# Loading batch 1 of a retention-and-mixer kernel through the casting software DMA queue, with ch2 weights queued later, ch1 of both halves first and u of batch 1 by crossbar

## The chip, the cores and the metric

One core of a Trainium2 chip. The time is the device time of one execution in microseconds; lower is better. Runs are compared with runs of the kernel before that were made on the same chip in the same job. Engines: PE is TensorE, DVE VectorE, ACT ScalarE, POOL GpSimd, SP SyncE. Lines are given as L with the number in the kernel's file; the changed kernel's numbers are 3 to 9 higher than those of the kernel before. "At half rate" or "cold" is said of TensorE's array when matmuls start twice as far apart as usual; the granted clock is the profile's column for it (1.00 is full, 0.50 half). A hole is a gap in TensorE's work beyond the usual spacing of its matmuls.

## The reference

A retention layer (a decayed running sum of k times v, read out by q) on 4 batches of 8 heads, 768 steps, head size 64, and then a token mixer and a channel mixer on the 512 joined channels:

```python
for t in range(S):
    state = gamma[None, :, None, None] * state + einsum('bhd,bhe->bhde', k[:, :, t], v[:, :, t])
    y[:, :, t] = scale * einsum('bhd,bhde->bhe', q[:, :, t], state)
# x: y with its heads joined, (4, 768, 512)
h  = maximum(xt @ w_tok1, 0) @ w_tok2        # xt: x transposed, d_tok = 256
u  = x + h transposed
h2 = maximum(u @ w_ch1, 0) @ w_ch2           # d_ch = 1536
return u + h2
```

Matrix products run in fp16 with fp32 sums.

## The kernel before

Everything is an `Op` with an estimated duration; `arrange()` puts all Ops in an order by these estimates, and the order on each engine is then fixed in the program. Per batch there are four `front` stages (one for each pair of heads: the retention, the token mixer, u) and one `back` (ch1 and ch2, the two matrix products of the channel mixer, each for two halves of the sequence). The back of batch b fills TensorE while the fronts of batch b+1 run. Batch 0's front has nothing to hide behind.

In batch 0 the rows come through the software queue, issued by GpSimd, which casts q and v to fp16 on the way. In later batches they come as fp32 through SyncE's queue, and GpSimd casts q and v:

```python
def load(nm):
    ...
    eng = nc.gpsimd if first and p else nc.sync
    dma = eng.dma_start(out=t, in_=rows.rearrange("h (c p) d -> p (h c) d", p=P))
    if b == 1:
        tc.add_manual_dep(dma.ins, wops["c1", 1].ins.ins.name, ...,
                          reason="the weights come first")
def cast(slot, nm):
    if first:
        ... return nc.gpsimd.dma_start(out=t, in_=...)      # casts
    ld = load(nm)
    ... nc.gpsimd.tensor_copy(t, src.tile...)
# ... cut
after = {(3, "v"): (("t1", 0), ("t2", 0))}
for p in range(NP):
    front(0, p)
queue += [wops[w] for w in (("c1", 0), ("c1", 1), ("c2", 0))]
```

What GpSimd does in each front: the fp16 copy of x (two halves), the triangular mask on some of the score tiles, and the fp16 copy of u (two halves):

```python
nc.gpsimd.tensor_copy(X16.tile[:, half(hf)], X.tile[:, half(hf), pc])          # x cast
nc.gpsimd.affine_select(out=M.tile, in_=M.tile, compare_op=ALU.is_ge, ...)     # mask
nc.gpsimd.tensor_copy(u, X.tile[:, half(hf), pc])                              # u cast
```

The scheduler models how many DMAs may be open on a queue, with one entry for each Op:

```python
RING = dict(SP=3, POOL=8)
if op.dma and len(ring[op.eng]) >= RING[op.eng]:
    start = max(start, ring[op.eng][-RING[op.eng]])
```

## Time and profile before

| | kernel before |
|---|---|
| time, median of 4 runs | 207.12 us (206.38 to 207.40) |
| the traced run | 205.84 us, span 204.1 us |
| TensorE busy | 192.3 us, 94% of the span |
| first ch1 matmul of batch 0 | 33.66 us |
| hole of TensorE at k of batch 1 | 2.98 us beyond the usual spacing |
| from the first ch1 matmul to the last matmul | 167.2 us |
| last add and store | 3.2 us |

The time is the sum of three: when ch1 begins, how long the rest takes on TensorE (the dense part), and the tail. The lines for this are in the prediction, which starts from 207.16, the median of the first three of the four runs.

### The profile page before, as it was taken

The numbers are of one execution on the slowest core, as the hardware profiler recorded it, in microseconds if no ns is written. First come the engines' busy times: TensorE is split into PE (matmuls) and PEld (weight loads), VectorE is DVE, ScalarE is ACT, GpSimd is POOL, SyncE is SP. The second block draws the span as 40 slices with busy tenths as digits, with TensorE's granted clock in tenths as the row PEclk, the third lists the DMA queues.
The fourth block names the chain that finished last, engine by engine and source line by source line (L and its number), as shares of the span: only waits on it lengthen the run. The fifth ranks groups of instructions, "written<-read, shape, count | busy, mean of one in ns | idle before, by whom it ended". The sixth has DMA issues, their size and how long they took to land.

```text
span 204.1 us, 4737 instructions
## 1 busy us (share of the span) xinstructions
PE 192.3 (94%) x1900; PEld 118.8 (58%) x1900; DVE 112.6 (55%) x285; ACT 97.4 (48%) x211; POOL 69.2 (34%) x116
## 2 busy tenths in 40 slices
PE   6598999769999999999999999999999999999993
PEld 2354796444577766676646656566557545545552
DVE  7499863016698889896296545947582021021021
ACT  7256797642489642465503650275115604604700
POOL 7998283033145543453442134215132000000000
PEclk9999999999999999999999999999999999999999
DMA  7999999989799999999997999898531112012012
GB/s 114 179 218 186 208 211 206 250 201 262 186 273 215 190 182 231 219 217 169 161 244 173 136 228 237 149 219 133 128 95 51 39 51 103 3 51 103 0 55 103
DMA packets 88470, 32.55 MB, mean 159 GB/s; under 512 B 79328, under 2 KB 84704, under 8 KB 88448
## 3 DMA queue, kind: packets, MB, share of 16 engines
q1 hardware_dynamic: 76128, 25.57, 61.3%
q0 software_dynamic: 12320, 6.69, 23.2%
q8 instruction: 15, 0.25, 0.5%
q14 instruction: 7, 0.06, 0.1%
HBM read 26.74 MB, written 6.29 MB: 162 GB/s over the span
## 4 chain that ended last, share of the span: by engine, by line
PE 81%; DMA 8%; DVE 6%; ACT 2%; issue 1%; POOL 0%; POOLq 0%; DVEq 0%
PE ba L626 31%; PE ba L597 28%; DMA kf<-in_k_dram 5%; PE fa L491 5%; PE fa L512 4%; PE fa L403 4%; DMA v<-in_v_dram 3%; PE fa L440 2%; DVE k L313 2%; PE fa L437 2%; PE fa L361 2%; DVE am L416 1%; PE fa L332 1%; ACT qT L340 1%; DVE U L373 1%
## 5 line engine op out<-in xcount | busy, mean ns | idle before, releaser
L626 PE MATMUL ba<-wc,h 128*128 128x512 f16 (+1 forms) x300 | 68.9, 371 | 0.0
L597 PE MATMUL ba<-uT,wc 128*128 128x384 f16 x384 | 68.2, 326 | 0.0
L610 ACT ACTIVATE h<-ba 128x384 f16<-128x384 f32 x96 | 46.4, 492 | 39.2 <-PE ba L597 38.7
L597 PEld LDWEIGHTS <-wc 128*128 128x128 f16 x384 | 36.0, 98 | 22.5
L626 PEld LDWEIGHTS <-h 128*128 128x128 f16 x300 | 27.2, 98 | 25.6
L635 DVE TENSOR_TENSOR o<-x,ba 128x512 f32<-128x512 f32 (+1 forms) x25 | 16.6, 663 | 42.1 <-PE ba L626 42.0
L416 DVE TENSOR_TENSOR am<-fa,mask 128x384 f16<-128x384 f32 x58 | 29.9, 551 | 11.8 <-PE fa L403 11.7
L468 POOL CAST x<-x 128x384 f16<-128x384 f32 x30 | 15.2, 514 | 28.2 <-issue 12.7
L519 DVE TENSOR_TENSOR x<-x,fa 128x384 f32<-128x384 f32 x28 | 14.5, 551 | 11.6 <-PE fa L512 11.2
L313 DVE TENSOR_SCALAR k<-kf,gk 128x384 f16<-128x384 f32 x32 | 15.8, 534 | 8.5 <-DMA kf<-in_k_dram 8.5
L451 ACT ACTIVATE x<-fa,gy 128x192 f32<-128x192 f32 (+1 forms) x42 | 14.9, 421 | 8.6 <-PE fa L440 8.6
L373 DVE SCALAR_TENSOR_TENSOR U<-U,gp,fa 128x64 f32<-128x64 f32 x64 | 17.5, 276 | 1.1
L292 POOL CAST q<-qf 128x768 f16<-128x768 f32 x12 | 10.2, 849 | 21.4 <-DMA qf<-in_q_dram 20.5
L380 ACT ACTIVATE r<-U 64x320 f16<-64x320 f32 x16 | 7.5, 466 | 20.6 <-DVE U L373 20.6
L530 POOL CAST u16w<-x 128x384 f16<-128x384 f32 x16 | 7.9, 508 | 20.9 <-DVE x L519 20.9
L440 PE MATMUL fa<-v,am 128*128 128x64 f16 x192 | 13.6, 193 | 0.0
L440 PEld LDWEIGHTS <-am 128*128 128x128 f16 x192 | 12.1, 98 | 2.3
L491 PEld LDWEIGHTS <-wt 128*128 128x128 f16 x192 | 11.9, 98 | 2.1
L512 PEld LDWEIGHTS <-wt 128*128 128x128 f16 x192 | 11.8, 98 | 2.2
L292 POOL CAST v<-vf 128x768 f16<-128x768 f32 x12 | 9.9, 827 | 8.6 <-DMA vf<-in_v_dram 7.9
L194 PE MATMUL fa<-zero 128*128 128x512 f16 x37 | 10.7, 423 | 2.2 <-DVE zero L52 1.3
L340 ACT COPY qT<-fa 128x768 f16<-128x768 f16 x8 | 11.5, 1443 | 2.1 <-PE fa L328 1.7
(60 smaller groups left out, 174.4 us busy)
## 6 DMA issues: line engine op xcount, KB each, us to landing
out_dram<-o SPq DMA_DIRECT2D x23, 256.0 KB, 2.3
kf<-in_k_dram SPq DMA_DIRECT2D x13, 384.0 KB, 6.4
qf<-in_q_dram SPq DMA_DIRECT2D x12, 384.0 KB, 5.8
vf<-in_v_dram SPq DMA_DIRECT2D x12, 384.0 KB, 5.3
wc<-in_moe_w_ch_dram POOLq DMA_DIRECT2D x1, 1536.0 KB, 24.3
kf<-in_k_dram POOLq DMA_DIRECT2D x3, 384.0 KB, 6.4
wc<-in_moe_w_ch_dram POOLq DMA_DIRECT2D x1, 1024.0 KB, 16.2
q<-in_q_dram POOLq DMA_DIRECT2D x4, 192.0 KB, 5.9
```

The source lines that it names most:

```text
L292: nc.gpsimd.tensor_copy(t, src.tile.rearrange("p (h c) d -> p h c d", h=2))
L313: (nc.gpsimd if keng == "POOL" else nc.vector).tensor_scalar(k16[:, :, j, :], src, gk[:, h:h + 1], None, ALU.mult)
L373: nc.vector.scalar_tensor_tensor(U[:, c], U[:, c - 1], gp[:, p:p + 1], o, ALU.mult, ALU.add)
L416: nc.vector.tensor_tensor(am, src[:, :HC], mask, ALU.mult)
L440: nc.tensor.matmul(o[:, j * D:(j + 1) * D], AM[2 * hf + j].tile[:, i], V.tile[:, j * NC + c], start=(c == 0), stop=(c == 0 or j == 1))
L468: nc.gpsimd.tensor_copy(X16.tile[:, half(hf)], X.tile[:, half(hf), pc])
L491: nc.tensor.matmul(acc[:, jt * P:(jt + 1) * P], wt1[:, i, jt * P:(jt + 1) * P], X16.tile[:, i], start=(i == 0), stop=(i == NC - 1))
L512: nc.tensor.matmul(acc[:, i * P:(i + 1) * P], wt2[:, jt, t], H1.tile[:, jt], start=(jt == 0), stop=(jt == NJ - 1))
L597: nc.tensor.matmul(acc[:, :SH], w[:, ct, f * P:(f + 1) * P], UT.tile[:, ct, sh * SH:(sh + 1) * SH], start=(ct == 0), stop=(ct == NP - 1))
L610: nc.scalar.activation(H2.tile[:, ft], A.tile[:, :SH], AF.Relu)
L626: nc.tensor.matmul(A.tile[:, :CW], H2.tile[:, ft, i * P:(i + 1) * P], wc2[:, ft, cs], start=(ft == 0), stop=(ft == NF - 1))
L635: nc.vector.tensor_tensor(o[:, :CW], X.tile[:, sh * HC + i, cs], A.tile[:, :CW], ALU.add)
```

## The change

The rows of batch 1 are to come through the casting queue as well. That frees them of the wait for the ch1 weights and of sharing the DMA engines with the ch2 weights, and GpSimd of its casts. The ch2 weights move between the second and third pair of batch 1; batch 0 does ch1 of both halves first, so that these weights are wanted later; u of batch 1 is transposed by a crossbar DMA (one that transposes on the way) and not on TensorE. q of batch 1 leaves the "long" form (three rows in one piece) and becomes two DMAs, one for each head.

```diff
-    LONG, XK, XQ, XU, XBAR = 2, 2, 2, 2, 1500
+    LONG, XK, XQ, XU, XBAR = 1, 2, 2, 1, 1200
-    FILL, TOKBA = 0.75, 2
+    FILL, TOKBA, PRE, TWICE, SOFT = 0.75, 2, 2, 1, 2
+        soft = b < SOFT
-                eng = nc.gpsimd if first and p else nc.sync
+                eng = nc.gpsimd if soft and (b or p) else nc.sync
-                if b == 1:
-                    tc.add_manual_dep(...)
-            if first:
+            if soft:
                 def emit():
                     t = tile_of(slot, sb, [P, 2 * NC, D], F16)
+                    if nm == "q" and b >= LONG:
+                        t = t.rearrange("p (c h) d -> p h c d", h=2)
+                        return [nc.gpsimd.dma_start(out=t[:, h], in_=rows[h].rearrange("(c p) d -> p c d", p=P))
+                                for h in range(2)][-1]
...
+        for part in ((ch1, 0), (ch1, 1), (ch2, 0), (ch2, 1)) if b < TWICE else (...):
+            part[0](part[1])
-    after = {(3, "v"): (("t1", 0), ("t2", 0))}
+    after = {(0, 3, "v"): (("t1", 0), ("t2", 0), ("c1", 0), ("c1", 1))}
+    after[... 1, PRE - 1, "v"] = ... + (("c2", 0),)
-    queue += [wops[w] for w in (("c1", 0), ("c1", 1), ("c2", 0))]
```

Cut: the estimates of some Ops, the order of the k casts, waits that only the scheduler sees, and the form of q's transposes: a q of a software-queue batch that is loaded in the long form is turned on TensorE in 12 matmuls of half width for each pair, any other in 6.

More of the change, by code (lines that the diff above doesn't have):

```diff
@@ L173, in arrange @@
                 shared = min(op.dma, both // 2)
+                if op.eng == "SP" and at > 5000:
+                    at, shared = max(at, free[other]), 0
                 free[mine] = at + op.dma + shared
@@ L210 @@
     weight(("c2", 0), 7800, wc2, moe_w_ch2)
-    queue, sp_done = [], [None]
+    queue, sp_done, kdone = [], [None], []
     x_add, uT_done, y_done, t1_done, t2_done = {}, {}, {}, {}, {}
@@ L256, in emit @@
                     dma = eng.dma_start(out=t, in_=rows.rearrange("h (c p) d -> p (h c) d", p=P))
-                if b == 1:
-                    tc.add_manual_dep(
-                        dma.ins, wops["c1", 1].ins.ins.name,
-                        mybir.DependencyInfo(mybir.DependencyClass.Sync, mybir.DependencyReason.DATA),
-                        reason="the weights come first")
                 return dma
             ns = QLONG if nm == "q" and b < LONG else 1750
-            if first and p:
-                o = Op("POOL", (0,), 1000, 1000, emit, [], [slot], dma=ns)
+            if soft and (b or p):
+                o = Op("POOL", (0,) if first else (2, b, p), 1000, 1000, emit, [], [slot], dma=ns)
                 queue.append(o)
@@ L268, in load @@
                 o = Op("SP", (0, b, p), 100, 100, emit,
-                       deps=[sp_done[-1]] + ([wops["c1", 1]] if b == 1 else []), takes=[slot], dma=ns)
+                       deps=[sp_done[-1], queue[-1] if b == SOFT and p == 0 else None], takes=[slot], dma=ns)
                 sp_done.append(o)
@@ L282, in emit @@
                     return nc.gpsimd.dma_start(out=t, in_=rows.rearrange("h (c p) d -> p (h c) d", p=P))
-                o = Op("POOL", (0,), 1000, 1000, emit, [], [slot], dma=QLONG if nm == "q" else 1400)
+                o = Op("POOL", (0,) if first else (2, b, p), 1000, 1000, emit, [], [slot],
+                       dma=QLONG if nm == "q" and b < LONG else 1400)
                 queue.append(o)
@@ L301, in front @@
                 base=0, pattern=[[0, HC], [1, P]], channel_multiplier=-1)))
-        if first:
-            queue.extend(wops[w] for w in after.get((p, "q"), ()))
+        queue.extend(wops[w] for w in after.get((b, p, "q"), ()))
         vc = cast(V, "v")
-        if first:
-            queue.extend(wops[w] for w in after.get((p, "v"), ()))
+        queue.extend(wops[w] for w in after.get((b, p, "v"), ()))
         def emit():
@@ L315, in front @@
         keng = "POOL" if first and p in KPOOL else "DVE"
-        kc = op(keng, 900, 980, emit, [kl], [K], [KF])
+        kc = op(keng, 900, 980, emit, [kl, kdone[-1] if b else None], [K], [KF])
+        kdone.append(kc)
         KT, QT = Slot("kT"), Slot("qT")
@@ L325, in emit @@
                 for c in range(NC):
-                    if src is Q and first:
+                    if src is Q and soft and b < LONG:
                         for j in range(2):
@@ L332, in emit @@
                     nc.tensor.transpose(tp[:, c * P:(c + 1) * P], o.rearrange("p h d -> p (h d)"), ident16)
-            t = op("PE", 340, 500, emit, [dep, t1_done.get(b * NP - 1) if b > 1 else None], [T], [src])
+            t = op("PE", 340, 500, emit, [dep, t1_done.get(b * NP - 1) if b > 0 else None], [T], [src])
             def emit():
@@ L349, in emit @@
                     in_=src.tile.rearrange("p c h d -> p (c h d)" if src is K else "p c d -> p (c d)"))
-            return Op("SP", (-1, b, p), 100, 100, emit, [dep], [dst], [src], dma=XBAR)
+            return Op("SP", (-1, b, p), 1220, 1220, emit, [dep], [dst], [src], dma=XBAR)
         kt = crossbar(K, KT, kc) if b >= XK else turn(K, KT, kc, "DVE" if first else "ACT")
@@ L362, in emit @@
                                      V.tile[:, j * NC + c], start=True, stop=True)
-        pp = op("PE", 300, 470, emit, [kc, vc, y_done.get(b * NP + p - 2), t1_done.get(b * NP - 1) if b > 1 else None], [ST], [K, V])
+        pp = op("PE", 300, 470, emit, [kc, vc, y_done.get(b * NP + p - 2), t1_done.get(b * NP - 1) if b > 0 else None], [ST], [K, V])
         prev = None
@@ L569, in front @@
             tk = [UT] if (b, "uT") not in uT_done else []
-            e = Op("SP", (-1, b, p), 100, 100, emit, [uc] + ([] if tk else [uT_done[b, "uT"]]), tk,
+            e = Op("SP", (-1, b, p), 1220, 1220, emit, [uc] + ([] if tk else [uT_done[b, "uT"]]), tk,
                    [UW] if tk else [UW, UT], dma=XBAR)
@@ L585, in op, with ch1 @@
             return Op(eng, ((1 if eng == "PE" else 0), b, seq[0]), occ, lat, emit, deps, takes, uses)
-        for sh in range(2):
+        halves = {}
+        def ch1(sh):
             H2 = Slot("h2")
@@ L612, in back, with ch2 @@
                               [A] if ft == 0 else [A, H2]))
+            halves[sh] = H2, rel
+        def ch2(sh):
+            H2, rel = halves[sh]
             for i in range(HC):
@@ L644, in back @@
                     st.prio, st.dma = (-2, b), 800 // parts
-    after = {(3, "v"): (("t1", 0), ("t2", 0))}
+        for part in ((ch1, 0), (ch1, 1), (ch2, 0), (ch2, 1)) if b < TWICE else ((ch1, 0), (ch2, 0), (ch1, 1), (ch2, 1)):
+            part[0](part[1])
+    after = {(0, 3, "v"): (("t1", 0), ("t2", 0), ("c1", 0), ("c1", 1))}
+    after[0 if PRE == 0 else 1, 3 if PRE == 0 else PRE - 1, "v"] = after.get((0 if PRE == 0 else 1, 3 if PRE == 0 else PRE - 1, "v"), ()) + (("c2", 0),)
     for p in range(NP):
         front(0, p)
-    queue += [wops[w] for w in (("c1", 0), ("c1", 1), ("c2", 0))]
     for b in range(1, B):
```

## The prediction

> **What bounds the kernel now.** I read the page first, then the busy times by stretch, the chain of waits, and the timelines of TensorE, GpSimd and SyncE in the first 60 us. The page gives TensorE 192.3 us of the 204.1 us span. By stretch (columns: stretch, its length, busy us of PE, PEld, DVE, ACT, POOL with counts, granted clock, DMA share, GB/s):
>
> ```profile
> 33.60:39.70 6.10, 6.08 (x41) 3.56 (x39) 0.00 (x0) 4.95 (x11) 0.29 (x1) 1.00 1.20 222
> 39.70:42.50 2.80, 0.01 (x1) 0.01 (x1) 0.75 (x2) 0.02 (x1) 0.00 (x0) 1.00 1.01 225
> 42.50:50.00 7.50, 7.50 (x65) 4.11 (x66) 2.52 (x7) 3.72 (x6) 3.31 (x4) 1.00 1.13 231
> 50.00:60.00 10.00, 10.00 (x115) 6.16 (x114) 8.22 (x22) 5.65 (x11) 2.03 (x3) 1.00 0.94 237
> 60.00:140.00 80.00, 80.00 (x895) 52.15 (x893) 58.46 (x143) 38.96 (x86) 32.76 (x57) 1.00 1.09 199
> 140.00:200.94 60.94, 60.90 (x414) 34.37 (x411) 16.63 (x34) 21.62 (x47) 5.29 (x10) 1.00 0.22 65
> ```
>
> The reader is to see three parts. Up to 33.6 us the front of batch 0 runs (a chain of short steps over all engines; ch1 of batch 0 needs all its u). From 33.6 TensorE is full, but for one hole of 2.8 us ending at 42.5. From 42.5 to 200.94 it is busy 158.40 of 158.44 us: nothing can be gained there except by taking matmuls away. The last 3.2 us are the last add and store. So the time is: when the dense part starts, plus the hole, plus the dense work.
>
> The chain of waits names the hole (start, us, what):
>
> ```profile
> 31.27 0.17 DVE x L519
> 31.45 10.21 DMA kf<-in_k_dram
> 41.68 0.76 DVE k L313 x2
> 42.49 0.51 PE fa L332 x6
> ```
>
> The first k rows of batch 1 are issued only when the second piece of the ch1 weights has landed, and then need 10.2 us. The front of batch 0 leans on GpSimd, whose timeline is (start, us, what, idle before):
>
> ```profile
> 12.88 1.54 POOL L203 DMA_DIRECT2D wt<-in_moe_w_tok_dram  x2
> 14.38 1.57 POOL L203 DMA_DIRECT2D wc<-in_moe_w_ch_dram  x2
> 18.85 1.84 POOL L420 TENSOR_SCALAR_AFFINE_SELECT am<-am 128x384 f16<-128x384 f16 x3 [0.87 <-ACT am L414]
> 24.50 0.95 POOL L468 CAST x<-x 128x384 f16<-128x384 f32 x2 [3.81 <-ACT x L451]
> 25.41 1.00 POOL L420 TENSOR_SCALAR_AFFINE_SELECT am<-am 128x384 f16<-128x384 f16 x2
> 26.35 0.50 POOL L468 CAST x<-x 128x384 f16<-128x384 f32 x1
> 28.33 2.09 POOL L530 CAST u<-x 128x384 f16<-128x384 f32 x4
> 31.96 1.93 POOL L530 CAST u<-x 128x384 f16<-128x384 f32 x4 [1.54 <-DVE x L519]
> ```
>
> It has one free gap, 20.7 to 24.5 us; after it come, without slack, the x casts, the masks and the eight u casts, and TensorE begins ch1 right behind (33.66 us in its timeline). Which weights land when, from the list of DMA issues (KB, us to landing):
>
> ```profile
> wc<-in_moe_w_ch_dram POOLq DMA_DIRECT2D x1, 1024.0 KB, 16.2
> wc<-in_moe_w_ch_dram POOLq DMA_DIRECT2D x1, 512.0 KB, 11.7
> ```
>
> The 1024 KB piece (second ch1 weights) is issued at about 15.2 us, so it lands at 31.4.
>
> **What the Trainium skill says.** (1) "DMA: Bandwidth & Descriptors", Queues, rings and completion order: an engine takes turns between queues packet by packet. The trace agrees: the k load took 10.2 us beside the ch2 weights in the other queue, and 3.6 us at best elsewhere. (2) The same page, Anatomy of one DMA: "any semaphore wait happens on the issuing sequencer before dispatch". The trace agrees; SyncE's queue stood with its second load until the weights were in:
>
> ```profile
> 0.81 31.02 SPq L256 DMA_DIRECT2D kf<-in_k_dram  x2
> ```
>
> (3) "TensorE: Matmul & The Clock Gate", Part 1: after about 3.4 us without work the array runs at half rate until some 3.4 us of work have passed. In the trace the first seven filler matmuls start 0.43 us apart, later ones 0.216; the hole of 2.8 us left no slow matmuls behind it. Its granted-clock column shows 1.00 all the same, so it will not show this.
>
> **The change part by part.**
>
> *k, q, v of batch 1 by the software queue.* Removed: the wait on the ch1 weights and the turns with the ch2 weights. In one queue, behind the ch1 weights, the rows of pair 0 come first: batch 0's pairs took 4.0 us each in the DMA records, so k of pair 0 should land near 33 us, v near 36, pair 1 by about 40. The hole should go: -2.98 us (the gap between two starts on TensorE, less the usual 0.16). Also removed: eight GpSimd casts of 0.83 us in batch 1; they sat on no critical step.
>
> Added: DMA issues on GpSimd, in its one instruction stream. k and v cost 1.03 us each in this trace. q, no longer in the long form, is two DMAs of 768 rows; the 768-row token weights cost 0.74, so about 1.5 us for both. A pair is 3.6 us. The built program puts pairs 0 and 1 (about 7 us) before the x cast of pair 1, the one that began at 24.5 us: the first k in the slot of the old ch2 issue, the rest in the 3.8 us gap. Already this overruns the gap by about 2.5 us.
>
> It is worse than that. The software queue's DMAs share eight semaphores in turn, and each issue waits until the DMA eight before it has landed. In the built program's GpSimd order, with waits:
>
> ```
> 36 L279 DMACopy q16_499<-in_q_dram 128x6x64 [waits DMASW4_49]
> 37 L279 DMACopy q16_499<-in_q_dram 128x6x64 [waits DMASW5_49]
> 38 L285 DMACopy v16_528<-in_v_dram 128x12x64 [waits DMASW6_49,PE_49]
> 39 L471 TensorCopy x16_547<-x_304 128x384 [waits Activation_49]
> ```
>
> The v load of pair 1 waits for DMASW6 at 32; its earlier users are q of batch 0's third pair and the 1024 KB weights. So it is issued when those land, at 31.4 us, and the x cast behind it, at 24.5 before, starts after 31.4 + 1.04 = 32.4. (The kernel's own schedule counts the two q DMAs as one and so believes in an earlier one.) From there GpSimd works in order: four x casts and three masks (7 x 0.48 = 3.3, to 35.8), u (0.5), the ch2 issue (1.0), three u (1.5), a k issue (1.0), three u (1.5): the seventh u, which ch1 waited for at about 33.4, is ready at 41.7. TensorE cannot go round it: its stream holds y of pair 2, which needs the first of those masks, next. ch1 starts at about 41.9 instead of 33.66: **+8.3 us**.
>
> *ch2 weights between pairs 1 and 2.* Issued near 36.5 us, they need 11.1 us of queue at most (their packets before: 25.2 to 36.3 in the records' own time, contended), so they land by 48 to 49. ch2 now comes after both ch1 halves: 96 matmuls x 0.163 = 15.6 us plus the front of batch 1 after 41.9, beyond 60. Hidden. Pairs 2 and 3 land by about 56; wanted near 60. Hidden, with 4 us to spare.
>
> *ch1 of both halves first.* The same matmuls in another order: no gain by itself; it buys the ch2 weights 7.8 us. It doubles ACT's share there: 24 relu of 0.49 = 11.8 us beside 15.6 us of ch1, stretched by the front of batch 1. Tight but possible.
>
> *u of batch 1 by crossbar.* 24 transposes leave TensorE, 6 in 0.34 us:
>
> ```profile
> 71.64 0.34 PE fa L543 x6
> ```
>
> -1.35 us, all on the path, as TensorE is full there. Four evictions of 0.8 us leave ACT and four crossbar transfers (3.3 us to landing) enter SyncE's queue.
>
> *q in plain form.* Four qT copies fall from 1.44 to about 0.8 us on ACT; off the path.
>
> **Sum.** -2.98 - 1.35 + 8.3 = +4.0. For new stalls in the static order and a cold array (TensorE idles about 6.5 us ahead of 33.4, over the 3.4 us), +1, an estimate. 207.16 + 5 = 212.
>
> **The rivals.** *A, the intended gain:* GpSimd's stall does not reach ch1, the hole and the transposes go: 207.16 - 4.3 = 202.8. For it: the hole is real. Against: a wait on an issuing queue blocks what stands behind it, as SyncE's 31 us show, and the x cast stands behind it. If only the length of the issues mattered (+2.5, and +2 for the two issues among the u casts), the time would be 207.4. *B, more than I say:* the static order, made for a front that ends sooner, or crossbars of batch 1 behind waiting stores on SyncE, opens holes in the dense part, and the array stays cold into ch1: 1 to 4 us more, 213 to 216. Against: after 41.9 all data of pairs 0 and 1 are in. *C, GpSimd's stall is shorter:* the ch1 weights land earlier, with no load on the other queue. Against: in the kernel before that queue was idle until they had landed too.
>
> **Range and chances.** The certain part is the stall until about 31.4; the x cast is late by 7 to 8, ch1 by 7 to 9. With gains of 3 to 4.3 and 0 to 3 of new holes: 209.9 to 214.9 by the extremes of each, widened below for A. 2% is at 211.3; I am a little above it. Predicted 212.0, range 207.5 to 215.5; faster 0.06, within 2% 0.35, slower 0.59.
>
> **What would show it.** GpSimd's timeline: the v issue standing until about 31.4, the x cast of pair 1 at 32.4, the last u near 42. TensorE: idle from about 27 to 33, ch1 from about 42, no wait for k of batch 1 after it, 158 us of dense work to the end, 24 transposes of u left. I am wrong if the x cast starts before 28, if ch1 starts before 38, or if TensorE shows more than 3 us of holes after ch1 has begun.

## The result

The changed kernel takes 212.04 us (median of 4 runs, 211.68 to 212.25) against 207.12. The ratio is 1.0242, 95% interval 1.0211 to 1.0272: 2.4% slower. A ratio here and below is the mean time of one kernel's runs over that of the other's of the same rounds, so not quite the ratio of the medians that are quoted. Executions over 1.5% slower than the fastest of the same kernel are left out of the means.

GpSimd's timeline of the changed kernel (start, us, what, idle before it and what ended that):

```profile
24.45 0.82 POOL L279 DMA_DIRECT2D q<-in_q_dram  x1 [0.57 <-DMA wt<-in_moe_w_tok_dram]
26.95 0.82 POOL L279 DMA_DIRECT2D q<-in_q_dram  x1 [1.69 <-DMA wc<-in_moe_w_ch_dram]
32.25 1.01 POOL L285 DMA_DIRECT2D v<-in_v_dram  x1 [4.48 <-DMA wc<-in_moe_w_ch_dram]
33.26 0.52 POOL L471 CAST x<-x 128x384 f16<-128x384 f32 x1
...
40.52 1.06 POOL L533 CAST u<-x 128x384 f16<-128x384 f32 x2 [1.23 <-DVE x L522]
42.59 1.85 POOL L533 CAST u<-x 128x384 f16<-128x384 f32 x4
```

The third line is the v load of batch 1's pair 1: GpSimd stood 4.48 us for the second piece of the ch1 weights (1024 KB) before it could issue that load, and 1.69 us for the first piece before the half of q ahead of it. The x cast right behind it had been at 24.50; it is at 33.26. The profile itself names the weights ("DMA wc") as what ended the wait, and so does the chain of waits (start, us, what):

```profile
15.04 16.68 DMA wc<-in_moe_w_ch_dram
...
33.26 0.52 POOL x L471
33.78 0.48 POOL am L423
```

TensorE's timeline in the same stretch:

```profile
26.20 0.19 PE L443 MATMUL fa<-v,am 128*128 128x64 f16 x1
34.30 0.24 PE L443 MATMUL fa<-v,am 128*128 128x64 f16 x1 [7.91 <-POOL am L423]
...
35.93 1.49 PE L494 MATMUL ba<-x,wt 128*128 128x128 f16 x12
...
44.23 0.65 PE L602 MATMUL ba<-uT,wc 128*128 128x384 f16 x3
```

TensorE stands 7.91 us in the middle of y of pair 2, for a mask (L423) that GpSimd does behind that x cast. ch1 begins at 44.23 instead of 33.66. The third line shows twelve matmuls in 1.49 us that took 0.83 before: the array is at half rate. The lines of the kernel before:

```profile
25.43 0.83 PE L491 MATMUL ba<-x,wt 128*128 128x128 f16 x12
33.66 0.65 PE L597 MATMUL ba<-uT,wc 128*128 128x384 f16 x3
```

Busy times by stretch, columns as in the prediction:

```profile
26.20:34.30 8.10, 0.20 (x4) 0.05 (x3) 0.56 (x1) 0.48 (x1) 2.87 (x5) 0.64 1.50 211
34.30:44.23 9.93, 9.37 (x129) 8.86 (x130) 5.33 (x10) 6.14 (x17) 7.92 (x15) 0.78 1.27 138
44.23:207.31 163.08, 163.07 (x1494) 98.66 (x1491) 88.76 (x204) 69.81 (x155) 43.90 (x72) 1.00 0.80 145
```

The granted clock falls to 0.64 and 0.78 in the first two stretches. From 44.23 on TensorE is full: 163.07 busy of 163.08 us, no gap over 0.12 us beyond the usual spacing, no wait for k of batch 1 and none for the ch2 weights. (GpSimd does stand a third time, 0.89 us for the ch2 weights before v of pair 3 at 50.6 us; nothing urgent was behind it.) So the change did what it was for (167.2 us of dense part became 163.1) and lost more than that ahead of it (33.66 became 44.23).

### The profile page after: what moved, and what is told of

It is laid out like the page before. It is cut to its first block, busy times and chain, and to the rows that moved or that the text cites.

```text
span 210.5 us, 4693 instructions
## 1 busy us (share of the span) xinstructions
PE 193.9 (92%) x1878; PEld 119.6 (57%) x1878; DVE 115.4 (55%) x285; ACT 92.6 (44%) x207; POOL 77.6 (37%) x124
## 4 chain that ended last, share of the span: by engine, by line
PE 80%; DMA 11%; POOL 5%; issue 2%; DVE 1%; POOLq 0%; DVEq 0%
PE ba L602 30%; PE ba L635 30%; DMA wc<-in_moe_w_ch_dram 8%; PE fa L494 4%; PE fa L515 4%; DMA v<-in_v_dram 3%; PE fa L406 3%; PE fa L443 3%; PE fa L440 2%; PE fa L364 2%; PE fa L335 1%; POOL kf L260 1%; POOL v L285 1%; POOL u L533 1%; PE ba L515 1%
## 5 line engine op out<-in xcount | busy, mean ns | idle before, releaser
L635 PE MATMUL ba<-wc,h 128*128 128x512 f16 (+1 forms) x300 | 67.5, 371 | 0.0
L644 DVE TENSOR_TENSOR o<-x,ba 128x512 f32<-128x512 f32 (+1 forms) x25 | 16.6, 665 | 43.3 <-PE ba L635 43.1
L533 POOL CAST u16w<-x 128x384 f16<-128x384 f32 x24 | 12.1, 518 | 27.7 <-DVE x L522 27.5
L443 PE MATMUL fa<-v,am 128*128 128x64 f16 x192 | 14.6, 198 | 7.9 <-POOL am L423 7.9
L443 PEld LDWEIGHTS <-am 128*128 128x128 f16 x192 | 13.0, 102 | 10.6 <-POOL am L423 8.1
L315 DVE TENSOR_SCALAR k<-kf,gk 128x384 f16<-128x384 f32 x32 | 17.1, 576 | 0.0
L197 PE MATMUL fa<-zero 128*128 128x512 f16 x42 | 12.2, 426 | 2.6 <-DVE zero L52 1.3
L515 PEld LDWEIGHTS <-wt 128*128 128x128 f16 x192 | 12.5, 101 | 2.4
L502 ACT ACTIVATE h<-fa 128x256 f16<-128x256 f32 x14 | 5.3, 380 | 19.0 <-PE fa L494 19.0
L494 PEld LDWEIGHTS <-wt 128*128 128x128 f16 x192 | 12.4, 102 | 1.8
L440 PE MATMUL fa<-r,qT 128*128 128x128 f16 x80 | 12.8, 227 | 0.3 <-DVE r L390 0.3
L515 PE MATMUL fa<-h,wt 128*128 128x128 f16 x168 | 12.2, 219 | 0.0
```

Of the source, the lines that this page charges most:

```text
L315: (nc.gpsimd if keng == "POOL" else nc.vector).tensor_scalar(k16[:, :, j, :], src, gk[:, h:h + 1], None, ALU.mult)
L440: nc.tensor.matmul(o, QT.tile[:, c * P:(c + 1) * P], R[:, c - 1], start=True, stop=False)
L443: nc.tensor.matmul(o[:, j * D:(j + 1) * D], AM[2 * hf + j].tile[:, i], V.tile[:, j * NC + c], start=(c == 0), stop=(c == 0 or j == 1))
L494: nc.tensor.matmul(acc[:, jt * P:(jt + 1) * P], wt1[:, i, jt * P:(jt + 1) * P], X16.tile[:, i], start=(i == 0), stop=(i == NC - 1))
L515: nc.tensor.matmul(acc[:, i * P:(i + 1) * P], wt2[:, jt, t], H1.tile[:, jt], start=(jt == 0), stop=(jt == NJ - 1))
L635: nc.tensor.matmul(A.tile[:, :CW], H2.tile[:, ft, i * P:(i + 1) * P], wc2[:, ft, cs], start=(ft == 0), stop=(ft == NF - 1))
```

## The experiments

The theory: in the program the DMAs of the software queue take eight completion semaphores in turn (in the trace numbers 103 to 110, over and over), so each issue waits until the DMA eight before it has landed. With q as two DMAs, v of pair 1 stands eight behind the 1024 KB ch1 weights. That wait sits in GpSimd's stream ahead of work that batch 0's front needs. Rivals: the time of the issues on GpSimd (about 1 us each) is the cost; two q DMAs cost by themselves; the cold array; the new order of halves; the crossbars. All twelve kernels gave correct results. The changed kernel's 212.04 was measured in another job than theirs; the kernel before had medians of 207.01 to 207.12 in all four jobs, so times are compared across them. Medians are over all four runs of a kernel; runs 7, 11 and 12 have one slow run each (208.80, 208.72 and 220.84).

| run | time, us (range) | kernel before, us | ratio to before (95%) | first ch1, us |
|---|---|---|---|---|
| changed kernel | 212.04 (211.68 to 212.25) | 207.12 | 1.024 (1.021 to 1.027) | 44.2 |
| 1 one q DMA | 204.00 (203.71 to 204.26) | 207.05 | 0.985 (0.979 to 0.992) | 34.9 |
| 2 one q DMA, GpSimd padded | 205.13 (204.27 to 205.84) | 207.05 | 0.991 (0.985 to 0.997) | 35.1 |
| 3 fillers | 211.73 (210.88 to 213.62) | 207.05 | 1.024 (1.017 to 1.032) | 42.1 |
| 4 loads behind u | 202.75 (202.54 to 202.80) | 207.05 | 0.979 (0.974 to 0.985) | 33.9 |
| 5 u on TensorE | 214.41 (213.50 to 214.44) | 207.01 | 1.037 (1.030 to 1.044) | 44.0 |
| 6 halves in turn | 213.13 (212.57 to 213.68) | 207.01 | 1.032 (1.026 to 1.038) | 44.9 |
| 7 before, u by crossbar | 207.20 (205.44 to 208.80) | 207.01 | 1.000 (0.993 to 1.008) | 32.6 |
| 8 two q DMAs behind u | 209.26 (208.42 to 210.44) | 207.01 | 1.014 (1.007 to 1.020) | 33.8 |
| 9 the same, ch2 weights later | 201.99 (201.72 to 202.17) | 207.01 | 0.976 (0.972 to 0.980) | 33.7 |
| 10 before again | 207.27 (one run) | 207.01 | | 33.1 |
| 11 k by crossbar too | 207.14 (205.54 to 208.72) | 207.01 | 0.999 (0.992 to 1.005) | 34.0 |
| 12 k and q by crossbar | 216.04 (215.40 to 220.84) | 207.01 | 1.043 (1.038 to 1.048) | 33.9 |

### 1. One q DMA: the wait goes, GpSimd's order stays

```diff
-    LONG, XK, XQ, XU, XBAR = 1, 2, 2, 1, 1200
+    LONG, XK, XQ, XU, XBAR = 2, 2, 2, 1, 1200
```

> The changed kernel with q of batch 1 in the long form, so that each q is one DMA of the software queue and not two; GpSimd's work stands in the same order. The v load of pair 1 then waits for the token weights (landed near 23.5 us) and not for the 1024 KB ch1 weights (31.7 us). Theory (the wait on the DMA eight before it is the cost): v is issued by 25.5, the x cast of pair 1 starts near 25.5 instead of 33.3, ch1 near 36.5 instead of 44.2, and the time is 204 to 206. Rival (the time of the DMA issues on GpSimd is the cost): only 2 x 0.84 us of issues go ahead of the x cast, ch1 near 42.5, time about 210.4.

GpSimd's timeline, v of pair 1 and the x cast:

```profile
24.48 1.06 POOL L285 DMA_DIRECT2D v<-in_v_dram  x1
25.49 0.56 POOL L471 CAST x<-x 128x384 f16<-128x384 f32 x1
```

No wait stands before v; the x cast is 7.8 us earlier than in the changed kernel, ch1 at 34.87, a little earlier than expected, and the time 204.00, 8.0 us below the changed kernel. The rival's 210.4 is out. The edit does one thing more than its expectation says: with q in the long form TensorE turns q of batch 1 in 48 matmuls of half width and not in 24 (1514 matmuls after ch1's start against 1490), and the dense part is 1.1 us longer (164.2 us against 163.1). So ch1 gains 9.4 us and the time only 8.0. The same holds for runs 2, 4 and 11.

### 2. The same with GpSimd's time kept

```diff
+                        if b == 1:
+                            nc.gpsimd.tensor_copy(pad, mask...)            # 128x384
+                            nc.gpsimd.tensor_copy(pad[:, :256], mask...)   # 128x256
```

> As the run before it, with two casts of 0.86 us in sum put on GpSimd behind each q of batch 1, so that GpSimd's own work ahead of the x cast is as long as in the changed kernel and only the wait is gone. Theory: the x cast starts near 27, ch1 near 38, time 205.5 to 207. Rival (issue time): as the changed kernel, 212.

```profile
25.07 1.03 POOL L290 DMA_DIRECT2D v<-in_v_dram  x1
26.09 0.52 POOL L476 CAST x<-x 128x384 f16<-128x384 f32 x1
```

The x cast comes at 26.09 and ch1 at 35.1, where 38 was expected. That is in the fastest of its runs (204.27), which is the one traced, and its front was 1.6 us ahead: its first q of batch 1 was issued at 19.30 against 20.94 in run 1. From that issue to the x cast it takes 6.8 us against 4.6, so the padding adds 2.2 us there. The time is 205.13, just under the range. By the medians GpSimd's own time is worth about 1 us and the wait about 7 of the 8; by the traces its own time could be up to 2.

### 3. Fillers for TensorE while it waits

```diff
+                if (b, p, hf) == (0, 2, 1):
+                    idle[0] = 35          # matmuls on zeros ahead of this y
```

> The changed kernel with 35 matmuls on zeros (7.6 us) put on TensorE where it waits for the mask of pair 2 (26.2 to 34.3 us), so that the array is not cold afterwards. GpSimd's stall stays. If the half-rate clock is a part of the loss: the granted clock stays at 1.00, the stretch from 34.3 to the first ch1 shrinks from 9.9 us by 0.7 to 1.5, time 210.5 to 211.4. If GpSimd and VectorE set that stretch: 212.0 as before.

```profile
34.00:42.07 8.07, 7.60 (x133) 6.91 (x132) 5.16 (x10) 6.04 (x17) 7.88 (x15) 1.00 1.43 148
```

The clock stays at 1.00. From the issue of v (32.00) to ch1 (42.07) it takes 10.1 us, against 12.0 in the changed kernel (32.25 to 44.23): the cold array is worth 1.9 us of the front, more than expected. The three waits of GpSimd for VectorE's adds (0.33, 0.37 and 1.23 us in the changed kernel) are gone with it. The time fell by 0.3 us only, less than expected, and its runs scatter over 2.7. In the trace 2.0 us of holes have come up at 98 to 150 us, two of them (1.0 us) at waits for the v casts of later batches on GpSimd. So the local gain is shown; why those loads came late in this order is not.

### 4. The loads of batch 1 behind the last u

```diff
-    LONG, XK, XQ, XU, XBAR = 1, 2, 2, 1, 1200
+    LONG, XK, XQ, XU, XBAR = 2, 2, 2, 1, 1200
-                o = Op("POOL", ..., emit, [], [slot], ...)
+                o = Op("POOL", ..., emit, [u_last[0] if b and (p > 1 or p == 1 and nm != "k") else None], [slot], ...)
```

> One q DMA, and from q of pair 1 on the software queue's loads of batch 1 and the ch2 weights stand behind the last u of batch 0 on GpSimd. Theory: the front of batch 0 is as in the kernel before (x cast near 24.5, ch1 near 33.7 to 34.5), no hole of TensorE at k of batch 1, 24 transposes fewer: 201.5 to 203. If the loads of pair 1 then come too late, a hole of 1 to 2 us follows ch1's start: 203 to 205.

```profile
24.74 0.95 POOL L471 CAST x<-x 128x384 f16<-128x384 f32 x2 [1.04 <-ACT x L454]
```

The x cast is at 24.74, ch1 at 33.90, no gap over 0.13 us follows, and the time is 202.75. The front of batch 0 is as before the change and the hole is gone: 4.3 us less than the kernel before. Fewer matmuls were expected, but from ch1 on there are as many as before (1514): 24 transposes of u leave, and q in the long form takes 24 more.

### 5 and 6. Parts of the change undone

```diff
-    LONG, XK, XQ, XU, XBAR = 1, 2, 2, 1, 1200
+    LONG, XK, XQ, XU, XBAR = 1, 2, 2, 2, 1200      # run 5: u of batch 1 on TensorE
-    FILL, TOKBA, PRE, TWICE, SOFT = 0.75, 2, 2, 1, 2
+    FILL, TOKBA, PRE, TWICE, SOFT = 0.75, 2, 2, 0, 2   # run 6: ch1, ch2, ch1, ch2
```

> The changed kernel with u of batch 1 turned on TensorE again (24 transposes and four evictions on ScalarE back, four crossbar transfers gone). By the prediction's term: 24 x 0.056 us more on a full TensorE, +1.35 us over the changed kernel, 213.4. If the crossbars made holes of their own, less than that or nothing.

> The changed kernel with ch1, ch2, ch1, ch2 by halves in batch 0 again. ch2 then wants its weights after 48 ch1 matmuls (7.8 us) and the front of one pair or two of batch 1 (3.4 us each), 55 to 59 us; they landed at 50.3 in the changed kernel. By the prediction nothing changes: 212 within 0.7. If the new order was needed for these weights: a hole before the first ch2 and 1 to 4 us more.

Run 5 is 2.4 us slower than the changed kernel, 1 us more than expected. Its dense part is 165.1 us against 163.1: 1.34 are the 24 transposes at 0.056, the other 0.7 lie in many small gaps and are not explained. Run 6 is 1.1 us slower, above its range. No hole stood before the first ch2, so the new order was not needed for the weights here, with ch1 11 us late. It was not undone in the good version, run 9. There it may be needed: ch2 began 17.1 us after ch1 in run 6, which in run 9 would be 50.8 us (an estimate), and run 9's ch2 weights landed at 53.4. 0.7 us is a later ch1 (44.95; GpSimd waited for the ch1 weights until 32.52 in that run), 0.6 a longer dense part.

### 7. The kernel before with u of batch 1 by crossbar

```diff
-    LONG, XK, XQ, XU, XBAR = 2, 2, 2, 2, 1500
+    LONG, XK, XQ, XU, XBAR = 2, 2, 2, 1, 1500
```

> The kernel before with u of batch 1 by crossbar and nothing else changed. TensorE is full from 42.5 us on, so 24 transposes fewer should show in full: -1.35 us, 205.7. If the crossbars queue behind stores on SyncE and ch1 of batch 1 waits for them: no gain or a loss.

No gain: 207.20 against 207.01, and a ratio of 1.000. The expectation of -1.35 fell. The traced run was the slow one (208.8), so its holes are not set against a fast run's. On its own this part is not worth its matmuls in the kernel before; in the changed kernel it is (run 5).

### 8 and 9. Two q DMAs, but behind u

```diff
-                o = Op("POOL", ..., emit, [], [slot], ...)
+                o = Op("POOL", ..., emit, [u_last[0] if b and (p > 1 or p == 1 and nm != "k") else None], [slot], ...)
-    FILL, TOKBA, PRE, TWICE, SOFT = 0.75, 2, 2, 1, 2
+    FILL, TOKBA, PRE, TWICE, SOFT = 0.75, 2, 3, 1, 2     # run 9 only: ch2 weights after pair 2
```

> As the run with the loads behind the last u of batch 0, but with two DMAs for each q as in the changed kernel: the number of DMAs, the eight semaphores and the issue times are those of the changed kernel, only the place of the issues in GpSimd's stream differs. Theory (a wait at that place in the stream is the cost, not the number of DMAs): ch1 near 34 us and 202.5 to 204. If two DMAs for q cost by themselves: over 206.

The time missed: 209.26, where the theory as written said 202.5 to 204. The front did what was expected (ch1 at 33.8). But the same wait came back in another place:

```profile
49.79 1.02 POOL L285 DMA_DIRECT2D v<-in_v_dram  x1 [5.58 <-DMA wc<-in_moe_w_ch_dram]
50.80 0.96 POOL L471 CAST x<-x 128x384 f16<-128x384 f32 x2
```

v of pair 3 stands eight DMAs behind the ch2 weights; GpSimd waits 5.58 us for them, the x cast of batch 1 waits behind it, and TensorE has a hole of 5.1 us at its first matmul on that cast, with half rate behind it (0.57 granted from 51.4 to 55.3). Run 9 moves the ch2 weights one pair on, so that no v is eight behind them:

> As the run with two q DMAs behind u, but with the ch2 weights queued after the third pair of batch 1, so that no v of batch 1 stands eight DMAs behind them. That run lost 5.6 us at 44.2 to 49.8 where v of pair 3 waited for the ch2 weights eight DMAs before it and the x cast of batch 1 stood behind it. Theory: that hole goes, GpSimd waits for no weights after 34 us, 202.5 to 204. If two q DMAs cost by themselves: 206 or more.

```profile
33.70:196.78 163.08, 163.08 (x1494) 98.47 (x1491) 88.94 (x203) 70.39 (x155) 48.73 (x77) 1.00 0.89 154
```

201.99 us, just below the range. ch1 begins at 33.70, and TensorE is full for 163.08 us. This is the best version, 2.4% under the kernel before and 4.7% under the changed one, with the changed kernel's DMAs and issue times. Only places in queues differ. The gain over the kernel before is clear of noise; whether it is over 2% is not (0.972 to 0.980). Against run 4 it is 0.8 us better, as its dense part is (163.1 against 163.9), which fits the 24 matmuls of q that the plain form saves.

### 10. The kernel before again

No edit.

> The kernel before once more, for its trace. Its runs fall in two groups, 204.9 to 206.0 us at a mean granted clock of 1.000 and 206.8 to 207.8 at 0.992; the trace that the prediction read is of the first. If the second is the array gone cold: a hole at k of batch 1 of over 3.4 us and ch1 matmuls 0.33 us apart behind it. If this run falls in the first group: hole of about 2.8 us and 0.163.

Busy times in the stretch behind the hole:

```profile
42.60:48.00 5.40, 5.40 (x28) 2.96 (x26) 0.00 (x0) 3.40 (x6) 2.49 (x3) 0.68 1.14 236
```

TensorE's timeline there:

```profile
42.25 0.51 PE L332 MATMUL fa<-ident,k 128*128 128x128 f16 x6 [3.16 <-DVE k L313]
42.60 3.34 PE L597 MATMUL ba<-uT,wc 128*128 128x384 f16 x12
```

The run took 207.27 us and is of the second group. Its hole is 3.32 us beyond the usual spacing, of which TensorE is idle for 3.16. That is under the 3.4 that was expected (the window in the prediction's third point from the skill), and the half rate came all the same. The twelve ch1 matmuls behind it take 3.34 us (2.11 in the trace that the prediction read), and the clock is at 0.68. The dense part is 169.3 us against 167.2. Of the 21 runs of the kernel before in the three experiment jobs, 15 had a mean clock of 0.992 and 206.7 to 207.9 us, and 6 a clock of 1.000 and 204.9 to 206.2. So in its usual run the kernel before pays about 5 us for the hole and its aftermath, and the trace at hand was the lucky kind. Each group has been traced once.

The clock records in the packed traces, which the views show only as means, tell more. Every stretch at half rate after the start and before the last matmul is 3.41 us long or two or three times that (3.41 in run 10, 10.24 in the changed kernel). Work at half rate loses half of its time, 1.7 us of 3.41, and the medians of the two groups lie 1.7 us apart (205.56 and 207.25). Counted in steps of 3.41 us from the first record of each of the 14 traces, the clock fell, or stayed low, at the end of every step in which TensorE was idle for 2.12 us or more (2.34 in run 10's, 39.91 to 43.32) and it fell after none with 1.98 or less (the trace that the prediction read, 38.24 to 41.65). By this count it matters where the hole falls, and not only how long it is. This is a pattern in these traces; no run moved a hole to test it.

### 11 and 12. k, then k and q of batch 1 by crossbar as well

```diff
-    LONG, XK, XQ, XU, XBAR = 2, 2, 2, 1, 1200
+    LONG, XK, XQ, XU, XBAR = 2, 1, 2, 1, 1200    # run 11, on run 4
-    LONG, XK, XQ, XU, XBAR = 1, 2, 2, 1, 1200
+    LONG, XK, XQ, XU, XBAR = 1, 1, 1, 1, 1200    # run 12, on run 9
```

> The version with one q DMA and the loads behind u, and k of batch 1 turned by crossbar as well (24 transposes of 0.056 us off TensorE, four evictions off ScalarE). If TensorE is full and the crossbars come in time: 1.3 us less than that version's 202.75, 201.4. If kT comes late: a hole after ch1's start, 203 or more.

> The version of the first run of this set (two q DMAs behind u, ch2 weights after pair 2) with k and q of batch 1 by crossbar. Against it 48 transposes of 0.056 us fewer: 2.7 us less if all crossbars come in time, 200 to 201.5; with holes in the front of batch 1 202 or more.

Both lost. Run 11 is 4.4 us above run 4 by the medians, 3.6 without its slow run (206.3). In its trace (206.3) TensorE has four large gaps after ch1's start, 4.3 us beyond the usual spacing: 1.5 us where q came late by DMA, 1.8 us at two places where v did, 1.0 us at a step of ScalarE. Run 12 reaches ch2 at 53.5 us, before its weights, which run 9's place in the queue had put late:

```profile
61.34 1.87 PE L637 MATMUL ba<-wc,h 128*128 128x512 f16 x4 [7.86 <-DMA wc<-in_moe_w_ch_dram]
```

That one wait is 7.9 of its 14 us over run 9. So run 12 says little about the crossbars themselves; with fewer matmuls ahead of ch2 the weights would have to come earlier, and that was not tried.

## Why the prediction was right, step by step

**The stall was right, and is shown.** v of pair 1 was to be issued at 31.4 us and was at 32.25; the x cast at 32.4 and was at 33.26, 8.8 us late where 7 to 8 was said. Run 2 takes the wait away and keeps GpSimd's work: about 7 us go with it, and 8 in run 1, which shortens that work too. Runs 8 and 9 make the same wait come and go in a second place.

**ch1's start: +8.3 predicted, +10.6 measured** (33.66 to 44.23). 0.85 us of the rest is the later issue: the weights landed at 31.7, and the issue began half a us after that. The larger part is the cold array, which the prediction had only in its "+1 for new stalls and a cold array". Run 3 measures it: 1.9 us. The prediction took GpSimd for the only thing that sets the stretch after the stall; with TensorE at half rate, VectorE's adds came late and GpSimd stood for them three times (0.33, 0.37 and 1.23 us). Run 3, at full rate, has none of these three waits. This is the mis-sized term, and ch1 lies outside the 7 to 9 us of the prediction's range. The prediction's own steps add up to 41.3 us for the seventh u and not 41.7, so to +7.9: with 0.85 for the later issue and 1.9 for the cold array that is 10.6.

**The hole: -2.98 predicted.** It went in full. But that was the size in a lucky trace; in the usual run it is about 2 us more with the half rate behind it (run 10). That size was wrong as well, and in the other direction: traced run against traced run the change costs 6.4 us (204.1 to 210.5), by the medians 4.9. The two errors nearly cancel, so 212.0 against 212.04 is partly luck. Nor do its parts give its upper figure: +9 for ch1, 3 gained and 3 of new holes make 216.2, and not 214.9.

**u by crossbar: -1.35.** The dense part fits: 167.24 - 2.98 - 1.34 = 162.9 against 163.07 measured. (The "158 us of dense work" in the prediction's last paragraph leaves out the 6 us of ch1 ahead of the hole.) Run 5 gives 2.4 us for undoing it, run 7 nothing for doing it alone. The term holds for the changed kernel; it is no constant.

**Hidden, as said:** the ch2 weights (landed at 50.3 us, first wanted at 70.0), pairs 2 and 3 (the last at 59.0), the order of halves. No gap over 0.12 us follows ch1's start, so rival B's new holes did not come, apart from the cold array. Rival A is out: the stall reached ch1. Its lesser form, that only the length of the issues matters, is out by runs 1 and 2. Rival C is out: the weights landed at 31.7 us (15.04 + 16.68 in the chain), no earlier.

**One statement was wrong:** that the granted-clock column would not show the half rate. It does (0.64 and 0.78). The 1.00 beside the slow fillers at the start of the first trace misled: that trace holds no clock record before 4.11 us, and the fillers become fast at 4.17.

Not settled: the 0.7 us of small gaps in run 5, why run 7 gained nothing, the late loads in runs 3 and 11, and whether run 9 needs the new order of halves.

## What to carry to other kernels

In these programs a DMA issue on GpSimd is an instruction in its stream like any other: look up which earlier DMA its semaphore belongs to, and what stands behind it. A load that nobody needs yet can stop a cast that everybody waits for, and a change in the number of DMAs shifts all later waits by one place. When a kernel's runs fall in two groups, find out which group the trace is of before a hole is priced from it.

## What the Trainium skill lacked or had wrong

- "DMA: Bandwidth & Descriptors" says that the wait is on the issuing sequencer. What such a wait costs the engine's compute behind it has no figure there, and that semaphores taken in turn make an issue wait for the DMA eight before it is on no page: GpSimd stood 4.48 us (changed kernel) and 5.58 us (run 8) with work behind the issue.
- The same page, Anatomy of one DMA, calls descriptor generation small and variable, without a figure by rows. Here an issue holds GpSimd for 1.03 us with 1536 rows, 0.82 with 768 and 0.77 in the long form: about 3.7 us for one pair's k, q and v.
- "TensorE: Matmul & The Clock Gate", Part 1, gives an idle window of about 3.4 us that runs freely (the page's table of advice says gaps of about 3 us), but not how idle a window has to be. TensorE stayed at full rate after a gap of 2.81 us (the first trace) and was at half rate after 3.16 us (run 10). In steps of 3.41 us, 2.12 us of idling brought half rate and 1.98 did not; the two times of the kernel before, 1.7 us apart, fit this.
- The same page warns that the clock's trace events are unreliable. Here the clock records agreed with the spacing of the matmuls wherever a gap had made the array cold (0.50 from 43.3 to 46.7 us in run 10); at the start of the program there is no record, and the column then shows 1.00.
